# Recurrent cross-attention and a softplus-erf MLP: more filler products at the start, the last stores over two queues, two copies ahead of a conversion step

## The chip, the core and the metric

The kernel runs on one core of a Trainium2 chip. A core has TensorE (PE, matrix products into PSUM), VectorE (DVE), ScalarE (ACT), GpSimd (POOL) and queues that issue DMA transfers, here the sync queue (SPq) and ScalarE's own (ACTq). The metric is the device time of one execution in microseconds; lower is better.

## What is computed

Eight batches with eight heads of 512 tokens by 64 numbers (x) and 32 state rows by 64 (state). Tokens read the states and states read the tokens, each through a softmax. The two results, 544 rows for each batch, are put side by side over the heads into rows of 512 numbers: 4352 rows. These go through a two-layer network.

```python
scores  = scale * x @ state.T;  a  = softmax(scores)      # 512 x 32, for each batch and head
xread   = a @ state
scores2 = scale * state @ x.T;  a2 = softmax(scores2)     # 32 x 512
sread   = a2 @ x
rows    = concat(xread, sread)                            # to (8 * 544, 8 * 64)
h       = rows @ w_in                                     # 512 -> 2048
out     = (h * erf(softplus(h))) @ w_out                  # 2048 -> 512
```

The data are float32, except that both weight matrices arrive as 64-bit floats and are turned into 32-bit ones on the chip.

## The kernel before

**How it is tiled.** Tokens stand in four quarters of 128 (index c), heads in four pairs (index i), the hidden width in four groups of 512 (index g). For tokens, rows @ w_in is not computed as written: for each batch the states are first multiplied with w_in (that is m, of 128 state rows by 2048), and h is then a @ m. For batches 1 to 7 and for the state rows at the end the products are built from seven instead of eight block products (`hidden7`, `project7`); batch 0 uses plain ones (`first0`, `project`).

**Batch 0 and the weights.** All of batch 0 up to line 907 is written out by hand, and `in_order` then ties the instructions of each engine to this order. While batch 0 is computed, 16 blocks of weights are fetched and converted, eight of w_in (kind "i") and eight of w_out (kind "o"). A block takes a DMA into one of three `raw` buffers, two steps on ScalarE (`on_act`, L144 and L146) and three on VectorE (`on_dve`, L147 to L149); the last of the three frees the buffer and so starts the next fetch.

**The opening.** x of batch 0 comes in four transfers, one for each quarter, in turn over ScalarE's and the sync queue (L109). `attention0` transposes the quarters on TensorE in the order 1, 0, 2, 3 (L302), four transposes each, into four PSUM tiles, which ScalarE and VectorE copy to SBUF (L305). One more transpose turns the states (L182, copied by L183). `scored` forms the scores (L197). Then VectorE goes through the softmax of the tokens (L217 to L235) and, at L319, makes `aT`, with the first block's conversion (L147 to L149) in between. `mixed_part` forms half a group of m from the states and w_in (L413) and ScalarE copies it (L415, L416). `first0` is the first product with a (L701); it needs both m and aT. `soft`, `keep_h`, `erf` and `times` make the activation, and `project` the second layer (L541).

**Filler.** `warm(n)` multiplies the identity by itself n times into a PSUM tile that nobody reads at that time (`spare`, L169). It is called before the first transposes and after the scores.

**Around line 809.** ScalarE first does both steps of w_out's block 4, then copies half of m for group 2 (`mixed_part(0, 2, 0, 2, ...)`), and then the transposed states of batches 1 to 7 (`states`, L183). VectorE's steps for that block come later.

**The end.** The last 256 rows are the state rows of all batches. `store7` adds up their results on VectorE (L601) in three pieces: left half of row block 0, whole row block 1, right half of row block 0. For each piece `put_s` issues four stores of 32 rows (L624), since the rows of different batches lie apart in the output. For row block 1 (r == 1) all four went to ScalarE's queue.

Of the kernel before, what the change touches and what calls it, by code (L numbers as in the profile page):

```python
# [16 lines left out]
def kernel(  # L17
# [17 lines left out]
    nc = tc.nc  # L35
# [130 lines left out]
    def warm(n):  # L166

        for _ in range(n):
            last = nc.tensor.matmul(out=spare[:, 0:P], lhsT=ident, rhs=ident, start=True,  # L169
                                    stop=True)  # L170
        return last
# [5 lines left out]
    def states(bs):  # L177


        ps = ps_h.tile([P, len(bs), P], F32, name="h")  # L180
        for k, b in enumerate(bs):
            last = nc.tensor.transpose(out=ps[:, k], in_=st[:, b, :], identity=ident)  # L182
        nc.scalar.copy(st[:, bs[0]:bs[-1] + 1, :], ps)  # L183
        return last
# [5 lines left out]
    def scored(b, xT):  # L190


        s2 = [ps_at.tile([P, S], F32, name="at") for _ in range(2)]
        for i in reversed(range(NI)):
            for e in range(2):
                r, q = slice(D * e, D * e + D), slice(Ns * i, Ns * i + Ns)
                on_pe = nc.tensor.matmul(out=s2[e][q, :], lhsT=st[r, b, q], rhs=xT[r, i, :],  # L197
                                         start=True, stop=True)
        marks.append(on_pe)
        return s2  # L200
# [10 lines left out]
    def states_weights(b, sc, both):  # L211

        aT[b] = keep.tile([P, 2, S], F32, name="aT")
        a = both[:, 0:2].rearrange("p e (k n) -> p e k n", n=Ns)
        m1 = small.tile([P, 2, NC * NI], F32, name="m1")
        for e in range(2):
            nc.vector.transpose(out=both[:, e], in_=sc[e])  # L217
        for e in range(2):
            nc.vector.reduce_max(out=m1[:, e], in_=a[:, e], axis=AX.X)
        for e in range(2):  # L220
            nc.vector.tensor_tensor(a[:, e], a[:, e], over(m1[:, e]), op=ALU.subtract)
            nc.scalar.activation(out=a[:, e], in_=a[:, e], func=ACTF.Exp, scale=scale)
        return a

    def sums(a):
        z1 = small.tile([P, 2, NC * NI], F32, name="z1")
        for e in range(2):
            nc.vector.reduce_sum(out=z1[:, e], in_=a[:, e], axis=AX.X)
        return z1

    def normalise(a, z1):
        nc.vector.tensor_scalar(z1, z1, 1e-9, None, op0=ALU.add)
        nc.vector.reciprocal(z1, z1)
        for e in range(2):
            nc.vector.tensor_tensor(a[:, e], a[:, e], over(z1[:, e]), op=ALU.mult)  # L235

    def largest(sc):
        m2 = small.tile([P, 2], F32, name="m2")
        for e in range(2):
            nc.vector.reduce_max(out=m2[:, e:e + 1], in_=sc[:, e], axis=AX.X)  # L240
        nc.vector.tensor_scalar(m2, m2, -scale, None, op0=ALU.mult)
        return m2

    def weigh_tokens(sc, m2, a2):

        z2 = small.tile([P, 2], F32, name="z2")
        for e in range(2):
            nc.scalar.activation(out=a2[:, e], in_=sc[:, e], func=ACTF.Exp, bias=m2[:, e:e + 1],
                                 scale=scale, accum_out=z2[:, e:e + 1])
        return z2  # L250

    def inverse(z):
        nc.vector.tensor_scalar(z, z, 1e-9, None, op0=ALU.add)
        nc.vector.reciprocal(z, z)

    def turn_weights(a2):
        a2T = att.tile([P, 2, NC, P], F32, name="sc")
        for e in range(2):
            ps = ps_at.tile([P, NC, P], F32, name="at")
            for c in range(NC):  # L260
                nc.tensor.transpose(out=ps[:, c, :], in_=a2[:, e, P * c:P * c + P],
                                    identity=ident)
            nc.scalar.copy(a2T[:, e], ps)
        return a2T
# [3 lines left out]
    def read_tokens(b, a2T, z2, pool=ps_at, name="at"):  # L268


        xt = x_t.pop(b)
        sr = pool.tile([P, 2, D], F32, name=name)
        for e in range(2):
            for c in range(NC):
                for i in reversed(range(NI)):
                    q = slice(Ns * i, Ns * i + Ns)
                    nc.tensor.matmul(out=sr[q, e, :], lhsT=a2T[:, e, c, q],  # L277
                                     rhs=xt[:, c, 2 * i + e, :],
                                     start=(c == 0), stop=(c == NC - 1))
        sn = sn_t[b] = const.tile([P, 2, D], F32, name="sn0") if b == 0 else \  # L280
            st[:, b - 1, :].rearrange("p (e d) -> p e d", e=2)
        for e in range(2):
            nc.vector.tensor_scalar(sn[:, e], sr[:, e], z2[:, e:e + 1], None, op0=ALU.mult)
# [8 lines left out]
    def attention0(between):  # L292

        xt = x_t[0]
        xT = att.tile([P, NI, S], F32, name="xT")
        xp = [ps_o.tile([P, S], F32, name="o%d" % i) for i in range(3)]
        xp.append(ps_h.tile([P, S], F32, name="h"))
        for c in 1, 0, 2, 3:  # L300
            for i in range(NI):
                nc.tensor.transpose(out=xp[i][:, P * c:P * c + P],  # L302
                                    in_=xt[:, c, 2 * i:2 * i + 2, :], identity=ident)
        for i in range(NI):
            (nc.scalar.copy, nc.vector.tensor_copy)[i % 2](xT[:, i, :], xp[i])  # L305
        states(range(1))
        s2 = scored(0, xT)
        between[0]()
        both = att.tile([P, NI, S], F32, name="xT")
        sc = att.tile([P, 2, S], F32, name="sc")  # L310
        a = states_weights(0, s2, both)
        for e in range(2):
            nc.scalar.copy(sc[:, e], s2[e])
        between[1]()
        z1 = sums(a)
        between[2]()
        normalise(a, z1)
        for e in range(2):
            nc.vector.transpose(out=aT[0][:, e], in_=both[:, e])  # L319

        def rest():
            a2 = both[:, 2:4]
            m2 = largest(sc)
            yield
            z2 = weigh_tokens(sc, m2, a2)
            inverse(z2)
            yield
            a2T = turn_weights(a2)
            yield
            read_tokens(0, a2T, z2)  # L330
            yield

        return rest()
# [71 lines left out]
    def mixed_part(b, g, j, parts, copy0=nc.scalar.copy, copy1=nc.vector.tensor_copy):  # L405
        n = gw // parts
        mg = m_t[b, g][:, :, n * j:n * j + n]
        fs = slice(2 * g + j, 2 * g + j + 2 // parts)
        ps = [ps_at.tile([P, gw], F32, name="at")[:, 0:n] for _ in range(2)]
        for i in range(NI):  # L410
            for e in range(2):
                r, q = slice(D * e, D * e + D), slice(Ns * i, Ns * i + Ns)
                nc.tensor.matmul(out=ps[e][q, :], lhsT=st[r, b, q],  # L413
                                 rhs=w_in[r, fs, i, :], start=True, stop=True)
        copy0(mg[:, 0], ps[0])  # L415
        copy1(mg[:, 1], ps[1])  # L416
# [202 lines left out]
    def put_s(r, ot, c=slice(0, d_model)):  # L619
        m = P // Ns  # L620
        for j in range(m):
            r0 = TB * (m * r + j) + S
            queue = nc.scalar if r == 1 or (c.start and j % 2) else nc.sync
            queue.dma_start(out=out[r0:r0 + Ns, c], in_=ot[Ns * j:Ns * j + Ns, c])  # L624

    def tiles(n):
# [4 lines left out]
    def begins(b):  # L631
        return 1 - b % 2
# [44 lines left out]
    def fetch():  # L677
        if len(made) < len(pieces):
            kind, j = w = pieces[len(made)]
            made[w] = (weights_in if kind == "i" else weights_out)(j)  # L680

    def on_act(kind, j, ks=range(2)):
        for k in ks:
            made[kind, j][0][k]()
# [34 lines left out]
    A, Z = slice(0, 2), slice(2, 4)  # L719
    for _ in range(3):  # L720
        fetch()
    warm(5)

    def after_scores():
        warm(28)
        on_act("i", 0)

    def before_sums():
# [3 lines left out]
    def amid_sums():  # L732
        on_dve("i", 0, [2])
        on_act("o", 0, [0])
        m_t[0, 0] = mix.tile([P, 2, gw], F32, name="m")
        mixed_part(0, 0, 0, 2, nc.scalar.copy, nc.scalar.copy)

    rest = attention0((after_scores, before_sums, amid_sums))
    g0 = group()
# [66 lines left out]
    on_dve("i", 4)  # L806
    times(Z, g1)
    on_act("i", 5)
    on_act("o", 4)
    some0(1, g1, range(NC), range(2))  # L810
    m_t[0, 2] = mix.tile([P, 2, gw], F32, name="m")
    mixed_part(0, 2, 0, 2, nc.scalar.copy, nc.scalar.copy)
    for bs in range(1, 5), range(5, B):
        states(bs)
    some0(1, g1, range(1), range(2, 4))
# [99 lines left out]
    for b in range(1, B + 1):  # L915
# [4 lines left out]
        for g, (first, second) in enumerate(groups):  # L920
# [5 lines left out]
            if b + 1 < B:  # L926
# [9 lines left out]
                if g > 1:  # L936
                    o = g - 2 ^ begins(b + 1)
# [56 lines left out]
```

## Time and profile before

| what | value |
|---|---|
| time, median of 3 | 736.64 us (736.46 to 736.71) |
| span of the profiled execution | 734.9 us |
| PE busy | 721.8 us (98%) |
| DVE busy | 523.8 us (71%) |
| ACT busy | 397.0 us (54%) |
| mean DMA rate | 63 GB/s |
| filler at L169 | 66 instructions, 275 ns at the median, up to 582 |
| first useful product (L701) starts at | 23.65 us |
| last addition (L601) starts at | 731.10 us |

PE's share is the time in which at least one product was in flight, not the share of its peak. The filler counts as busy too. The profile's order of time gives each instruction, or a run of equal ones, with its start, its duration, its engine and line, what it writes and reads, and in brackets how long the engine had idled and what ended the wait. Lines of the code are those of the kernel before; in the changed kernel they stand two to four lower.

### The profile page before, as it was taken

To read this page: it belongs to the slowest core of one execution; us is meant where nothing else is said; L and a number is where in the kernel's file an instruction comes from. 1 tells how busy PE (TensorE), PEld (TensorE's weight loads), DVE (VectorE), ACT (ScalarE), POOL (GpSimd) and SP (SyncE) were. 2 spreads that over 40 slices of the span, in tenths; PEclk is the share of its full clock that TensorE was granted. 3 is DMA by queue.
4 is the path that set the end of the run, shared out by engine and by line. 5 is a ranking of instruction groups with operands and counts; after the bars stand their busy time and mean duration, and the time that the engine had idled before them with its cause. 6 is when DMAs were issued, how large, how long until landed. Compare 5 with 4: busy or idle time off the path is not lost.

```text
span 734.9 us, 12066 instructions
## 1 busy us (share of the span) xinstructions
PE 721.8 (98%) x4986; PEld 586.4 (80%) x4986; DVE 523.8 (71%) x765; ACT 397.0 (54%) x499; POOL 0.7 (0%) x6
## 2 busy tenths in 40 slices
PE   7899999999999999999999999999999999999997
PEld 6434435887889888988989888988898899999996
DVE  3987887898698666867688568867686756575423
ACT  3899884657455545654355445654565434443340
POOL 0000000000000000000000000000000000000000
PEclk9999999999999999999999999999999999999999
DMA  7568752331142201510061104210121000000001
GB/s 232 172 202 251 209 110 58 87 58 18 41 89 59 45 11 34 111 29 29 1 144 21 38 1 87 61 35 21 27 62 29 30 1 29 1 29 1 29 1 29
DMA packets 139166, 46.40 MB, mean 63 GB/s; under 512 B 126696, under 2 KB 130536, under 8 KB 139112
## 3 DMA queue, kind: packets, MB, share of 16 engines
q1 hardware_dynamic: 136744, 44.78, 24.5%
q10 hardware_dynamic: 2368, 0.85, 0.6%
q8 instruction: 39, 0.64, 0.4%
q14 instruction: 15, 0.12, 0.1%
HBM read 33.03 MB, written 8.91 MB: 57 GB/s over the span
## 4 chain that ended last, share of the span: by engine, by line
PE 86%; DVE 5%; ACT 3%; issue 1%; DMA 0%; SPq 0%; ACTq 0%; DVEq 0%
PE o L591 48%; PE h L485 25%; PE o L541 5%; PE at L399 2%; PE h L399 1%; PE h L701 1%; PE at L197 1%; PE h L277 1%; DVE hs L493 1%; PE at L413 1%; ACT raw L146 1%; DVE raw L567 1%; ACT L711 1%; DVE s L536 1%; DVE hs L708 0%
## 5 line engine op out<-in xcount | busy, mean ns | idle before, releaser
L591 PE MATMUL o<-w_out,s 128*128 128x256 f32 x480 | 118.2, 380 | 0.9 <-DVE ot L601 0.5
L591 PE MATMUL o<-raw,hs 128*128 128x256 f32 x480 | 117.0, 382 | 0.0
L492 ACT ACTIVATE s<-hs 128x512 f32<-128x512 f32 x120 | 75.3, 630 | 76.0 <-DVE hs L493 75.7
L591 PE MATMUL o<-w_out,hs 128*128 128x256 f32 x480 | 114.0, 380 | 0.2 <-DVE hs L590 0.2
L591 PEld LDWEIGHTS o<-raw,hs 128*128 128x128 f32 x480 | 90.0, 190 | 22.5 <-issue 10.9
L493 DVE TENSOR_TENSOR hs<-hs,h 128x512 f32<-128x512 f32 x90 | 61.7, 687 | 63.7 <-PE h L485 63.7
L591 PEld LDWEIGHTS o<-w_out,hs 128*128 128x128 f32 x480 | 90.6, 190 | 16.8 <-issue 4.2
L591 PEld LDWEIGHTS o<-w_out,s 128*128 128x128 f32 x480 | 84.6, 191 | 9.2 <-DVE ot L601 0.7
L493 DVE TENSOR_TENSOR hs<-s,h 128x512 f32<-128x512 f32 x60 | 41.0, 683 | 68.9 <-PE h L485 68.4
L485 PEld LDWEIGHTS h<-aT,m 128*128 128x128 f32 x672 | 83.9, 192 | 4.7 <-issue 1.4
L485 PE MATMUL h<-aT,m 128*128 128x128 f32 x672 | 84.7, 275 | 0.2 <-ACT s L496 0.2
L536 DVE TENSOR_TENSOR s<-s,hs 128x2048 f32<-128x2048 f32 x30 | 68.5, 2284 | 19.9 <-ACT s L535 19.9
L496 ACT COPY s<-h 128x512 f32<-128x512 f32 x29 | 17.0, 586 | 113.3 <-PE h L485 113.3
L541 PE MATMUL o<-w_out,s 128*128 128x512 f32 x128 | 59.0, 600 | 0.6 <-DVE s L714 0.5
L485 PE MATMUL h<-sy,sx 128*128 128x128 f32 x448 | 59.1, 275 | 0.0
L501 ACT COPY hs<-h 128x512 f32<-128x512 f32 x29 | 17.0, 586 | 76.1 <-PE h L485 76.1
L485 PEld LDWEIGHTS h<-sy,sx 128*128 128x128 f32 x448 | 56.6, 192 | 1.8 <-issue 0.5
L535 ACT ACTIVATE s<-s 128x2048 f32<-128x2048 f32 x30 | 57.4, 1912 | 0.3
L591 PE MATMUL o<-raw,s 128*128 128x256 f32 x240 | 56.8, 379 | 0.0
L541 PEld LDWEIGHTS o<-w_out,s 128*128 128x128 f32 x128 | 23.1, 190 | 30.7 <-issue 25.8
L591 PEld LDWEIGHTS o<-raw,s 128*128 128x128 f32 x240 | 43.5, 190 | 4.8
L492 ACT ACT_TABLE_LOAD x31 | 39.8, 1283 | 0.5
(130 smaller groups left out, 912.1 us busy)
## 6 DMA issues: line engine op xcount, KB each, us to landing
raw<-in_moe_w_in_dram SPq DMA_DIRECT2D x8, 1024.0 KB, 5.6
raw<-in_moe_w_out_dram SPq DMA_DIRECT2D x8, 1024.0 KB, 4.8
xq<-in_x_dram SPq DMA_DIRECT2D x112, 64.0 KB, 2.2
x<-in_x_dram SPq DMA_DIRECT2D x56, 128.0 KB, 2.9
out_dram<-ot SPq DMA_DIRECT2D x18, 256.0 KB, 2.1
sc<-xT SPq DMA_DIRECT2D x112, 32.0 KB, 1.9
out_dram<-ot SPq DMA_DIRECT2D x28, 128.0 KB, 1.7
x<-in_x_dram ACTq DMA_DIRECT2D x2, 256.0 KB, 5.7
```

Source lines behind the costliest of these rows:

```text
L146: lambda: nc.scalar.activation(out=lo, in_=lo, func=ACTF.Copy, scale=2.0 ** -29)], \
L197: on_pe = nc.tensor.matmul(out=s2[e][q, :], lhsT=st[r, b, q], rhs=xT[r, i, :], start=True, stop=True)
L399: nc.tensor.matmul(out=ps[k][e][q, :], lhsT=st[r, b, q], rhs=w_in[r, 2 * g:2 * g + 2, i, :], start=True, stop=True)
L485: last = nc.tensor.matmul(out=bank[:, q], lhsT=lhsT, rhs=rhs, start=(first and i == 0 and k == 0), stop=(i == GF - 1 and k == len(ops) - 1 ...
L492: nc.scalar.activation(out=s[:, k], in_=hs[:, k], func=ACTF.Softplus)
L493: add = lambda o, x, y: nc.vector.tensor_tensor(o, x, y, op=ALU.add)
L496: copy(m1, p)
L501: copy(c11, p)
L535: return (nc.scalar.activation(out=s, in_=s, func=ACTF.Erf), nc.vector.tensor_tensor(s, s, hs, op=ALU.mult))
L536: nc.vector.tensor_tensor(s, s, hs, op=ALU.mult))
L541: nc.tensor.matmul(out=acc[r], lhsT=gT[:, i, P * r:P * r + P], rhs=w_out[:, GF * g + i, :], start=(g == 0 and i == 0), stop=(g == NG - 1 a ...
L591: nc.tensor.matmul(out=acc[bank][:, E2 * c:E2 * c + E2], lhsT=lhs[:, i, :], rhs=rhs[:, g, i, :], start=(first and i == 0 and c == 0), stop ...
```

## The change

It has three parts. Filler: five products before the first transposes become eight, three more come ahead of the third quarter's transposes, 28 after the scores become 32, and five more follow the first half group of m. Their purpose is to keep TensorE at work while it waits. Stores: of the four stores of row block 1 the even ones go to the sync queue, so that both queues share them. ScalarE's order: the second step of w_out's block 4 moves behind the two copies of m, so that m is there earlier. What is computed stays the same.

```diff
         for c in 1, 0, 2, 3:
+            if c == 2:
+                warm(3)
             for i in range(NI):
                 nc.tensor.transpose(out=xp[i][:, P * c:P * c + P],
...
-            queue = nc.scalar if r == 1 or (c.start and j % 2) else nc.sync
+            queue = nc.scalar if j % 2 and (r == 1 or c.start) else nc.sync
...
-    warm(5)
+    warm(8)
 
     def after_scores():
-        warm(28)
+        warm(32)
         on_act("i", 0)
...
         mixed_part(0, 0, 0, 2, nc.scalar.copy, nc.scalar.copy)
+        warm(5)
...
     on_act("i", 5)
-    on_act("o", 4)
+    on_act("o", 4, [0])
     some0(1, g1, range(NC), range(2))
     m_t[0, 2] = mix.tile([P, 2, gw], F32, name="m")
     mixed_part(0, 2, 0, 2, nc.scalar.copy, nc.scalar.copy)
+    on_act("o", 4, [1])
     for bs in range(1, 5), range(5, B):
         states(bs)
```

## The prediction

> **What bounds the kernel now.** I read the chain that ended last, to see which engine sets the end and where it doesn't. It is TensorE nearly everywhere:
>
> ```profile
> PE 86%; DVE 5%; ACT 3%; issue 1%; DMA 0%; SPq 0%; ACTq 0%; DVEq 0%
> ```
>
> No edit touches the steady stretch that makes up this 86%. All four places lie in the first 66 us or the last 7, so I read the order of time there. The opening (columns: start us, duration us, engine, line, operation, tiles; the bracket is idle time before and what ended it; x is the number of instructions, and one 128x128 float32 product is two of them, a transpose one):
>
> ```profile
> 1.35 2.50 PE L169 MATMUL o<-ident 128*128 128x128 f32 x10 [1.35 <-POOL ident masks.py:199]
> ...
> 4.92 0.90 PE L302 MATMUL o<-ident,x 128*128 128x128 f32 x3 [1.06 <-DMA x<-in_x_dram]
> ...
> 7.96 0.90 PE L302 MATMUL o<-ident,x 128*128 128x128 f32 x3 [1.08 <-DMA x<-in_x_dram]
> ...
> 10.15 0.68 DVE L305 COPY xT<-h 128x512 f32<-128x512 f32 x1
> ...
> 10.98 1.96 PE L197 MATMUL at<-xT,st 64*32 64x512 f32 x16 [0.83 <-DVE xT L305]
> ...
> 12.87 8.34 PE L169 MATMUL o<-ident 128*128 128x128 f32 x56
> 13.12 1.31 DVE L217 STREAM_TRANSPOSE xT<-at 128x512 f32<-128x512 f32 x2 [2.29 <-PE at L197]
> ...
> 19.86 1.22 DVE L149 SCALAR_TENSOR_TENSOR w_in<-raw,w_in 128x1024 uint32<-128x1024 uint32 x1
> ...
> 21.22 0.79 PE L413 MATMUL at<-w_in,st 64*32 64x256 f32 x16
> ...
> 22.80 1.29 DVE L319 STREAM_TRANSPOSE aT<-xT 128x512 f32<-128x512 f32 x2
> 23.65 3.67 PE L701 MATMUL h<-aT,m 128*128 128x512 f32 x8 [1.64 <-DVE aT L319]
> ```
>
> The reader is to see a chain: x lands, transposes (L302), copies (L305), scores (L197), and then VectorE, busy without a pause from 13.12 to 24.09, which releases the first useful product at 23.65. TensorE is not the bound after 12.87: its 56 instructions at L169 are filler, and it idles 1.64 us before L701. Whatever makes the transposes and scores end sooner moves the start of VectorE's chain, and with it all that follows. TensorE also ran at half rate for most of this. Two pieces of its order of time, from inside the filler:
>
> ```profile
> 13.67 1.70 PE L169 MATMUL o<-ident 128*128 128x128 f32 x7
> ...
> 16.81 1.39 PE L169 MATMUL o<-ident 128*128 128x128 f32 x11
> ```
>
> The row for L169 gives one instruction 421 ns for most of the slow ones and 275 ns at the fast rate, so starts are (1.70 - 0.421) / 6 = 0.213 us apart before and (1.39 - 0.275) / 10 = 0.1115 us after: nearly twice as fast from about 16.7 us on. The page's clock row stays at 9 throughout and doesn't show this. The transposes also take 421 ns each, the slow figure; the same form at 84 us (L261) takes 272. Scores take 1.96 us here and, at the fast rate,
>
> ```profile
> 528.69 1.09 PE L197 MATMUL at<-xT,st 64*32 64x512 f32 x16
> ```
>
> So the first scores lose 0.87 us to the slow clock.
>
> [...]the clock rose about 3.85 us after the filler began at 12.87, and not earlier, though before that TensorE had work in 68 to 76% of every 3.4 us (busy 2.34, 2.32 and 2.57 us in 3.0 to 6.4, 6.4 to 9.8 and 9.8 to 13.2). [...]L701 starts 0.43 us apart, the full rate. [...]The trace shows that issue time: 0.41 to 0.44 us for a store at L624.
>
> **The change part by part.** Compared in order, the two kernels differ on the engines in nothing but these places.
>
> 1. **Filler before the first transposes, 5 to 8, and 3 between the second and third quarter.** Does it delay them? Eight products are 16 instructions: the second starts at 1.72, each 0.213 later, so the last one ends at about 4.93, when x lands (4.92). The eight transposes that follow take 8 x 0.213 and end at 6.64; three products at the slow rate, 6 x 0.213 = 1.28, end at 7.92, before the next quarter of x (7.96). Cost: nothing, the wait for x hides both. What they give: TensorE streams without a break from 1.35 to 9.9, which is 8.6 us[...] I take full clock by about 6.5.
>  - Transposes after 7.96: eight at 0.1115 instead of 0.213. The last one VectorE's first copy needs (the sixth) starts at 8.52 instead of 9.08 and takes 0.272 instead of 0.421: the copies start 0.70 us earlier. ScalarE's copies gain about 0.60, and with the small copy L183 end at 9.97, still before VectorE's at 10.13. Gain 0.70.
>  - Scores: 1.09 instead of 1.96. Gain 0.87.
>  - VectorE's chain then starts at 13.12 - 1.57 = 11.55. Does another wait take over? ScalarE's first conversion (L144, L146) waits for the weights and ends at 13.55; the exponentials behind it on ScalarE would be due at 16.31 - 1.57 = 14.74. VectorE's L147 and L148 read it at 15.15 and 15.96. None binds. The last of the first three weight blocks has landed by about 16 (DMA traffic falls to nothing there) and is read at 20.41 - 1.57 = 18.84. So the gain stands: 1.57 us.[...]
> 2. **Filler after the scores, 28 to 32.** Queued behind it on TensorE: L413, which needs w_in from L149, done at 21.08 - 1.57 = 19.51. At full rate 64 x 0.1115 = 7.1 us from about 11.2 ends at 18.3. Cost: nothing, hidden by VectorE's conversion.
> 3. **Five after L413.** Queued behind: L701, due at 23.65 - 1.57 = 22.08. L413 ends at about 20.2, the five end 1.1 us later at 21.4. Cost: nothing, hidden by VectorE's chain. They shorten the idle stretch.
> 4. **Copies of m ahead of a conversion step, at 64 us.** The order of time:
>
> ```profile
> 63.10 1.17 ACT L144 ACTIVATE w_out<-raw 128x1024 f32<-128x1024 f32 x1
> ...
> 64.18 1.15 ACT L146 ACTIVATE raw<-raw 128x1024 uint32<-128x1024 uint32 x1
> ...
> 65.22 0.34 ACT L415 COPY m<-at 128x256 f32<-128x256 f32 x1
> 65.46 0.36 ACT L416 COPY m<-at 128x256 f32<-128x256 f32 x1
> ...
> 65.73 0.97 ACT L183 COPY st<-h 128x512 f32<-128x512 f32 x2
> ...
> 66.37 1.98 PE L701 MATMUL h<-aT,m 128*128 128x512 f32 x4 [0.48 <-ACT st L183]
> ```
>
>  m would be ready 1.04 us sooner (its products are done at 63.25), but L701 is released by L183, and ahead of L183 stand the same three instructions in another order. VectorE's L148 needs L146, which would end at about 65.8 instead of 65.3; it starts at 66.44 behind L147. Gain and cost: nothing; L183 hides it.
> 5. **Last stores.** Before:
>
> ```profile
> 728.77 3.60 SPq L624 DMA_DIRECT2D out_dram<-ot  x6
> ...
> 730.10 2.77 ACTq L624 DMA_DIRECT2D out_dram<-ot  x6
> 731.10 0.42 DVE L601 TENSOR_TENSOR ot<-ot,o 128x256 f32<-128x256 f32 x1 [0.71 <-PE o L591]
> ```
>
>  The last half rows are ready at 731.52. ScalarE's queue is then still issuing its fourth whole-row store (to 731.9), and its last two start at 731.98 and 732.43. With two of the four moved to the sync queue, ScalarE's queue is free at 731.0; the sync queue issues its two after its first four (to 730.5) and is free at 731.4. Both then wait for 731.52, and the last issue starts at about 731.97. Gain 0.45. Unknown is how four stores at once land (1.5 to 1.9 us before): bounds 0.3 and 0.5.
>
> Does the early gain last? From 20 us to 160 us no compute engine's wait was ended by a DMA, and the transfers are started by buffers that come free, so all of it should shift together. Sum: 1.57 + 0.45 = 2.02, so 736.64 - 2.02 = **734.6 us**.
>
> **The rivals.** *The clock rises late, at the scores*[...]: 0.87 + 0.45, so 735.3.[...] *The clock rises where it did*: then eight more filler instructions end at 21.9, L413 and the five new products behind it end at 23.85, and L701 is 0.2 late: 736.64 + 0.2 - 0.45 = 736.4.[...] *The clock rises early and falls again* in the idle stretch from 18.3 to 19.5 and 21.4 to 22.1: L701's first eight instructions at half rate would take 3.4 us more, 736.64 - 2.0 + 3.4 = 738.0, slower than before. Against it: from 20.0 to 23.4 TensorE was busy for only 2.0 us, and the clock held.
>
> **How the numbers follow.** Forecast 70%, late rise 12%, no earlier rise 12%, fall 6%. The forecast spreads from 734.1 (the scores' and the stores' gains both a little larger) to 735.0; with the late rise the range reaches 736.0, and leaves out 18%. A change of 0.2% is 1.47 us, so faster means below 735.17: nearly all of the forecast and a third of the late rise, 0.70. Slower is the fall: 0.06. The rest, 0.24, is within.
>
> **What would show it.** In the profile after: transposes in the third quarter 272 ns instead of 421; scores in 1.09 us; VectorE's L217 at 11.5; L413 released by L149 and no longer behind filler; L701 at 22.1, still released by aT; L183 near 65.7 - 1.6; last stores issued by 732.4 less the shift, on both queues. Transposes still at 421 and L217 after 12.5 would prove the first step wrong; L701 at 0.85 us apart, the third.

## The result, and the profile after

The changed kernel takes 734.86 us (median of 6 runs, 734.77 to 734.94), beside 736.67 for the kernel before: 1.81 us less. The ratio is 0.9973, with a 95% interval of 0.996 to 0.9986. The forecast was 734.6.

The order of time of the changed kernel, opening. Lines of the code stand two to four lower than before (L304 is L302, L415 is L413, L703 is L701, L321 is L319):

```profile
1.35 3.65 PE L169 MATMUL o<-ident 128*128 128x128 f32 x16 [1.35 <-POOL ident masks.py:199]
...
4.84 0.51 PE L304 MATMUL o<-ident,x 128*128 128x128 f32 x3
...
5.98 0.83 PE L169 MATMUL o<-ident 128*128 128x128 f32 x6
7.84 0.55 PE L304 MATMUL o<-ident,x 128*128 128x128 f32 x3 [1.03 <-DMA x<-in_x_dram]
...
10.18 1.09 PE L197 MATMUL at<-xT,st 64*32 64x512 f32 x16 [0.65 <-DVE xT L307]
11.21 7.41 PE L169 MATMUL o<-ident 128*128 128x128 f32 x64
11.46 1.31 DVE L217 STREAM_TRANSPOSE xT<-at 128x512 f32<-128x512 f32 x2 [1.42 <-PE at L197]
...
19.56 0.79 PE L415 MATMUL at<-w_in,st 64*32 64x256 f32 x16 [0.94 <-DVE z L232]
...
20.27 1.38 PE L169 MATMUL o<-ident 128*128 128x128 f32 x10
...
21.14 1.30 DVE L321 STREAM_TRANSPOSE aT<-xT 128x512 f32<-128x512 f32 x2
21.99 3.67 PE L703 MATMUL h<-aT,m 128*128 128x512 f32 x8 [0.33 <-DVE aT L321]
```

The reader is to see that the eight first products end as x lands, that three transposes take 0.51 us where they took 0.90, that scores take 1.09 us where they took 1.96, and that VectorE's chain (L217) starts 1.66 us sooner. The first useful product keeps this lead (23.65 to 21.99), and so does the last addition, some 707 us later (731.10 to 729.45). L415 waited 0.94 us for VectorE, so none of the new filler stood in its way; L703 is still released by aT. The first transposes already run at the fast rate (0.51 us for three, 0.90 before): the trace has the granted clock at 1.00 from 4.73 us on, just ahead of the landing of x at 4.84.

At 64 us, ScalarE and the product behind it:

```profile
62.50 0.37 ACT L417 COPY m<-at 128x256 f32<-128x256 f32 x1
62.75 0.39 ACT L418 COPY m<-at 128x256 f32<-128x256 f32 x1
...
63.01 1.18 ACT L146 ACTIVATE raw<-raw 128x1024 uint32<-128x1024 uint32 x1
...
64.07 0.96 ACT L183 COPY st<-h 128x512 f32<-128x512 f32 x2
...
64.71 1.98 PE L703 MATMUL h<-aT,m 128*128 128x512 f32 x4 [0.49 <-ACT st L183]
```

L183 and the product start 1.66 us earlier than before (65.73 to 64.07, 66.37 to 64.71), which is the lead of the opening, and the product waits for L183 as it did. The new order itself moved nothing. The end:

```profile
727.11 3.70 SPq L626 DMA_DIRECT2D out_dram<-ot  x8
...
728.44 2.33 ACTq L626 DMA_DIRECT2D out_dram<-ot  x4
729.45 0.42 DVE L603 TENSOR_TENSOR ot<-ot,o 128x256 f32<-128x256 f32 x1 [0.71 <-PE o L593]
```

The last issue is over at 730.81 on the sync queue, 1.36 us after the last addition began; before it was over at 732.87 on ScalarE's, 1.77 after. That is 0.41 us. But the span, from 734.9 to 733.0, fell by only about 0.2 more than the addition's lead of 1.65.

### The profile page after: what moved, and what is told of

It is laid out like the page before. It is cut to its first block, busy times and chain, and to the rows that moved or that the text cites. A ratio compares the mean times of both kernels' runs of the same rounds, so it can differ in the third digit from the quotient of the medians.

```text
span 733.0 us, 12127 instructions
## 1 busy us (share of the span) xinstructions
PE 721.4 (98%) x5016; PEld 587.0 (80%) x5016; DVE 523.7 (71%) x765; ACT 397.0 (54%) x499; POOL 0.7 (0%) x6
## 4 chain that ended last, share of the span: by engine, by line
PE 87%; DVE 6%; ACT 2%; issue 1%; DMA 0%; SPq 0%; DVEq 0%; ACTq 0%
PE o L593 48%; PE h L487 26%; PE o L543 6%; PE at L401 2%; PE h L401 1%; PE h L703 1%; PE at L197 1%; PE at L415 1%; PE h L277 1%; DVE hs L495 1%; DVE raw L569 1%; DVE s L538 1%; DVE s L716 0%; DVE hs L710 0%; DMA out_dram<-ot 0%
## 5 line engine op out<-in xcount | busy, mean ns | idle before, releaser
L593 PEld LDWEIGHTS o<-w_out,hs 128*128 128x128 f32 x480 | 90.6, 190 | 16.8 <-issue 4.2
```

Source lines behind the costliest of these rows:

```text
L593: nc.tensor.matmul(out=acc[bank][:, E2 * c:E2 * c + E2], lhsT=lhs[:, i, :], rhs=rhs[:, g, i, :], start=(first and i == 0 and c == 0), stop ...
```

## The experiments

Each kernel was timed beside the kernel before on the same chip; figures are medians. The groups of experiments ran on different chips, on which the kernel before took 736.59 to 736.74 us (736.67 beside the changed kernel), so a difference to the changed kernel is known to some 0.1 us only. Of each run the mean granted clock of TensorE is on record too. It counts the time before the first change of the clock as full (the kernel before reads 1.00 from 13.2 to 16.6 us, where its products start 0.213 us apart, and they do so 0.1115 apart after 16.8), so it shows falls and not late rises; by my estimate 3.41 us at 0.50 take about 0.002 from it (3.41 x 0.50 / 735).

**The parts, each alone on the kernel before.** The four filler edits:

```diff
-    warm(5)
+    warm(8)
...
+            if c == 2:
+                warm(3)
...
-        warm(28)
+        warm(32)
...
         mixed_part(0, 0, 0, 2, nc.scalar.copy, nc.scalar.copy)
+        warm(5)
```

> Kernel before with the four filler edits alone (8, 3, 32 and 5 products); stores and ScalarE's order as before. My theory: the early rise of TensorE's clock gives nearly the whole gain; VectorE's L217 starts near 11.5 us instead of 13.12 and the time is 1.6 to 1.7 us below the kernel before (735.0). Rival, that the stores give a good part as forecast (0.45) and the filler the rest: 1.3 to 1.4 us below.

Measured: 735.15 us beside 736.74, ratio 0.9973 (0.9962 to 0.9983). L217 starts at 11.56. The filler is worth 1.6 us of the 1.81.

```diff
-            queue = nc.scalar if r == 1 or (c.start and j % 2) else nc.sync
+            queue = nc.scalar if j % 2 and (r == 1 or c.start) else nc.sync
```

> Kernel before with the last stores over both queues alone. From the two traces I expect 0.2 us less than the kernel before: the last issue comes 0.4 us earlier, and 0.2 of it is lost[...]. The forecast's figure was 0.45. Rival, that the stores give nothing: 0.0.

Measured: 736.42 us, 0.32 less at the median, ratio 0.9994 (0.9986 to 1.0002). The interval holds 1, so these times alone don't prove a gain. That the filler alone stays 0.29 above the whole change (0.22, each against its own kernel before) points the same way. The traces settle it: from the start of the last addition (L601) to the end of the span it is 3.8 us in the three with the old stores (kernel before, filler alone, ScalarE's order alone) and 3.5 to 3.6 in the two with the new ones (changed kernel, stores alone). The stores are worth 0.2 us.

```diff
-    on_act("o", 4)
+    on_act("o", 4, [0])
...
     mixed_part(0, 2, 0, 2, nc.scalar.copy, nc.scalar.copy)
+    on_act("o", 4, [1])
```

> Kernel before with the copies of m ahead of the conversion step alone. My theory: no change, within 0.1 us, since the first product of group 2 is still released by the copy of the states at L183, which ends at the same time. Rival, that m's earlier copy lets TensorE start group 2 sooner: up to 0.5 us less.

Measured: 736.66 us, ratio 0.9996 (0.9988 to 1.0004): no change that can be told. In its trace the first product of group 2 is again released by L183.

**The first eight alone.**

```diff
-    warm(5)
+    warm(8)
```

> Kernel before with eight instead of five filler products before the first transposes and nothing else (28 after the scores, none elsewhere). My theory: [...]the clock rises at about 4.7 us and the whole filler gain is there: 1.6 to 1.7 us below the kernel before. Rival 1, that the three products between the quarters are needed to keep the clock up: it falls before the scores, scores take 1.96 us, gain at most 0.8. Rival 2, that the first product needs the five fillers ahead of it: L701 starts 0.85 us apart.

Measured: 736.62 us, from 736.09 to 737.86, ratio 0.9997 (0.9989 to 1.0005). Eight alone bring nothing at the median and make the time uneven. The granted clock was 0.994 to 0.998 in all 13 runs, lower in each of them than in the six runs of the changed kernel, where it was 0.999 or 1.000. The profiled run, at 737.47 one of the three slowest, shows where. It is cut at the points where its granted clock changes (10.11, 13.52, 23.76 and 27.18), and the time between and before them into equal lengths (columns: stretch, length, TensorE busy with its instructions, granted clock, DMA share, GB/s):

```profile
6.70:10.11 3.41, 1.53 (x10) 1.00 1.10 346
10.11:13.52 3.41, 3.26 (x22) 0.50 1.05 417
13.52:16.93 3.41, 3.41 (x33) 1.00 0.46 185
16.93:20.35 3.42, 2.38 (x22) 1.00 0.00 0
20.35:23.76 3.41, 1.61 (x18) 1.00 0.68 202
23.76:27.18 3.42, 3.42 (x5) 0.50 0.26 105
```

The clock had risen by 7.91, where three transposes took 0.55 us, 0.85 at 5.79. It was 0.50 from 10.11 to 13.52 and from 23.76 to 27.18, and 1.00 from 13.52 to 23.76. In the stretches just ahead of the two at 0.50, TensorE was busy for 1.53 and 1.61 us. The scores took 1.96 us, as in the kernel before, and the first products

```profile
22.93 5.37 PE L701 MATMUL h<-aT,m 128*128 128x512 f32 x8 [1.64 <-DVE aT L319]
```

5.37 us in place of 3.67. Both of my rivals were right in this run and my theory wrong: with the eight the clock rose before the third quarter, but without the rest of the filler it did not stay up. Which part of the rest matters is the question of the next runs.

**Taking one place away from the changed kernel.**

```diff
-    warm(8)
+    warm(5)
```

> Changed kernel with five instead of eight products before the first transposes. My theory[...]: TensorE then streams without a break only from 4.9 to about 9.9 us[...]. Times spread between 735.0 and 736.5, more than the changed kernel's 0.2 us; median near 735.8. Rival[...]: no spread, 0.2 to 0.6 above the changed kernel.

Measured: 735.30 us, 14 runs from 734.77 to 736.55: the spread that I expected, with a lower median. The profiled run is the slowest of them: transposes still at 0.90 us for three, scores at 1.96, L217 at 13.18; the 64 filler instructions that start at 12.93 took 8.11 us, the changed kernel's 7.41. No run shows a fall (0.999 or 1.000 in all 14).

```diff
-            if c == 2:
-                warm(3)
```

> Changed kernel without the three products ahead of the third quarter's transposes. My theory: the clock rises by about 6.6 us in about half of the executions and then falls again before the scores[...]; scores take 1.96 us in most, and the time is 0.8 to 1.6 above the changed kernel (735.7 to 736.5). Rival, that eight products are enough: same as the changed kernel, 734.9.

Measured: 734.95 us, but in two heaps: 8 runs from 734.77 to 734.98 and 5 from 735.81 to 736.44, nothing between. I expected most of them in the higher heap. The profiled run is of the lower one, at a clock of 1.000. The record tells the heaps apart: the granted clock was 0.999 or 1.000 in all eight runs of the lower heap, 0.995 in four of the higher and 0.998 in the fifth. So the clock fell in the higher heap; where it fell, no trace shows.

```diff
-        warm(5)          # after the first half group of m
```

> Changed kernel without the five products after the first half group of m. My theory: in some 8 of 10 executions [...]the clock falls, and the first products at L701 run at half rate for up to 3.4 us; time 0.8 to 1.7 above the changed kernel in those (735.7 to 736.6), none above in the others. Rival[...]: 734.9.

Measured: 734.95 us, again two heaps: 7 runs from 734.75 to 735.05 and 3 from 735.95 to 736.21. I expected 8 in 10 in the upper one. The granted clock was 1.000 in all seven and 0.998 in the three. In the profiled run, from the lower, TensorE waited 0.95 us ahead of L415 and 1.64 ahead of L703, and the granted clock stayed at 1.00:

```profile
17.68:21.09 3.41, 1.69 (x25) 1.00 0.26 30
21.09:24.51 3.42, 2.55 (x6) 1.00 0.70 277
```

Here TensorE was busy for 1.69 of 3.41 us and the next stretch was at 1.00; in the run with eight alone it was 1.61, and the next stretch was at 0.50. What parts the two heaps, these traces don't show.

The kernel before has this gap too (TensorE waits 1.64 us ahead of L701), and its runs fall into two heaps as well: of the 96 taken beside these experiments, 8 took 738.0 to 738.2 us at a clock of 0.998, the others at most 736.9 at 0.999 or 1.000. Of the 20 runs with all four filler edits (changed kernel, filler alone, swapped order below) none shows a fall. So the new filler probably removes these longer executions too, but no trace of one was taken, and 20 runs are few. The step from 28 to 32 was never taken back alone.

**No filler after the scores, and none at all.**

```diff
-        warm(32)
...
-        warm(5)          # after the first half group of m
```

> Changed kernel without any filler after the scores and after the first half group of m (the eight and the three ahead stay). My theory: the clock rises early, VectorE's chain starts at 11.5 as in the changed kernel, but TensorE is nearly idle from 11 to 22 us, the clock falls in every execution and L701 (L703 there) starts at half rate; 1.5 to 2.6 us above the changed kernel (736.4 to 737.5), with little spread between early and late. Rival, that VectorE and ScalarE hide the slow products: under 0.5 us above.

Measured: 737.02 us (736.43 to 737.78), 2.2 above the changed kernel. The granted clock was 0.990 to 0.993 in all 13 runs, so it fell in every one. The stretches of the profiled run, cut at the changes, and the first products:

```profile
10.08:13.49 3.41, 1.09 (x16) 1.00 1.05 391
13.49:27.15 13.66, 6.26 (x22) 0.50 0.39 132
```

```profile
22.12 6.17 PE L703 MATMUL h<-aT,m 128*128 128x512 f32 x8 [1.20 <-DVE aT L321]
```

The granted clock was 0.50 from 13.49 to 27.15; the first products took 6.17 us instead of 3.67.

With every call of `warm` taken out of the changed kernel:

> Changed kernel with no filler anywhere. My theory: transposes and scores at half rate as in the kernel before (1.6 us) and the first products at half rate as well (1.5 to 2.6): 3.1 to 4.2 us above the changed kernel, 738 to 739. Rival, that the kernel before's own filler was worth nothing: 736.3, the kernel before less the stores' gain.

Measured: 738.49 us (737.78 to 739.12), 3.6 above the changed kernel, inside the expected 3.1 to 4.2.

**One DMA for each piece of the last rows.**

```diff
-        for j in range(m):
-            r0 = TB * (m * r + j) + S
-            queue = nc.scalar if j % 2 and (r == 1 or c.start) else nc.sync
-            queue.dma_start(out=out[r0:r0 + Ns, c], in_=ot[Ns * j:Ns * j + Ns, c])
+        rows = out.rearrange("(b t) e -> b t e", t=TB)[m * r:m * r + m, S:S + Ns, c]
+        queue = nc.scalar if r == 1 else nc.sync
+        queue.dma_start(out=rows, in_=ot[:, c])
```

> Changed kernel with each piece of the last rows stored by one DMA in place of four (three issues in all, over the two queues). My theory: what is left after the last addition is one issue of about 0.4 us and one landing of 1.5 to 2.0; the second issue on each queue (0.45 us) goes, so 0.3 to 0.5 less than the changed kernel, 734.4. Rival, that landing and not the issue sets the end: the same as the changed kernel within 0.1, or slower if one DMA of four times the size lands later.

Measured: 739.29 us, ratio to the kernel before 1.0034 (1.0022 to 1.0046), 4.4 above the changed kernel. The last addition starts at 729.46, as in the changed kernel, and the last issue is over at 730.5, so it is all in the landing. From 730.5 to 735.5 the DMA engines were busy 0.24 of the time, at 72 GB/s; the changed kernel's last stores, from 729.9 to 732.1, made 0.47 and 139 GB/s. Of the 16 engines that the profile counts, that is the work of about four (0.24 x 16), beside seven or eight (0.47 x 16). What makes the merged transfers slower, no run shows.

**A better order of the quarters.** By the changed kernel's trace the fourth quarter of x lands before the third (7.2 and 7.8 us).

```diff
-        for c in 1, 0, 2, 3:
-            if c == 2:
+        for c in 1, 0, 3, 2:
+            if c == 3:
                 warm(3)
```

> Changed kernel with the third and fourth quarters' transposes in the other order, since the fourth quarter of x lands at 7.2 us by the trace and the third at 7.8. My theory: with the clock up, four transposes (0.44 us) leave the path, but the states' copy, whose data land at 9.1, then holds the scores: 0.1 to 0.3 below the changed kernel. Rival: the copies, not the transposes, set the start of the scores, no change.

Measured: 734.55 us (734.41 to 734.66), ratio to the kernel before 0.9971 (0.9959 to 0.9982); 0.31 below the changed kernel's median (0.27, each against its own kernel before), with no run of either in the other's range. L217 starts at 11.24 instead of 11.46.

```diff
     for c in range(NC):
         (nc.scalar, nc.sync)[c % 2].dma_start(
             out=x_t[0][:, c], in_=x[0, :, P * c:P * c + P].rearrange("h p d -> p h d"))
-    for e in range(2):
-        nc.sync.dma_start(out=st[:, 0, D * e:D * e + D], ...
+        if c == 1:
+            for e in range(2):
+                nc.sync.dma_start(out=st[:, 0, D * e:D * e + D], ...
```

> As the swapped order, and the states' two small loads issued ahead of the fourth quarter of x. My theory: the states land in time and the full 0.44 us leaves the path: 0.35 to 0.45 below the changed kernel, 734.45. Rival: the fourth quarter, issued 1 us later, lands after the third, and nothing or less than the swap alone is gained.

This stands on top of the swapped order. Measured: 735.79 us (735.57 to 737.31), 0.9 above the changed kernel and 1.2 above the swapped order: the rival was right, and the loss was larger than it said. The profiled run is the slowest of the 13. In it the fourth quarter came late, TensorE waited 1.92 us,

```profile
8.92 0.79 PE L305 MATMUL o<-ident,x 128*128 128x128 f32 x3 [1.92 <-DMA x<-in_x_dram]
```

and from 9.08 on the granted clock was 0.50 (stretches cut at the changes):

```profile
5.67:9.08 3.41, 1.49 (x13) 1.00 1.17 306
9.08:12.49 3.41, 2.58 (x17) 0.50 1.06 411
12.49:15.91 3.42, 3.42 (x26) 0.50 0.70 284
```

The scores then took 1.96 us, and L217 started at 13.96, where the swapped order had 11.24. Its transposes waited until 8.92 for the load, where the swapped order began them at 7.67: 1.25 us later at the load became 2.7 at L217. This is the worst case and not the usual one. Nine of the 13 runs took 735.57 to 735.90 at a clock of 0.999 or 1.000, three 736.28 to 736.45 at 0.998, and the profiled one 737.31 at 0.995. The fall of the clock thus goes with the spread and not with the median, whose loss of 1.2 us against the swapped order is about the lateness of the load alone.

## Why the prediction held, step by step

1. *The filler hides in the waits for x, and the clock rises early.* Right. The eight end with the landing of x and the three before the third quarter. The clock rose at 4.73 us. That it would be up by about 6.5 was an estimate of mine; nothing in the trace of the kernel before showed it. L217 moved 1.66 us, forecast 1.57. The copies gained 0.80 (forecast 0.70; the third quarter landed 0.12 earlier in this run, 7.84 for 7.96), the scores and what waits for them 0.86 (forecast 0.87). In the traces of the filler alone, of the swapped order, without the five and without filler after the scores, whose loads and filler up to there are the same, the clock rose later: three transposes of the first two quarters took 0.85 to 0.88 us, and from 7.6 us on 0.49 to 0.55:

```profile
4.93 0.85 PE L304 MATMUL o<-ident,x 128*128 128x128 f32 x3
```

 This is from the swapped order, against 0.51 in the changed kernel. It costs little, because the quarter that follows is awaited anyway: L217 started at 11.56, 11.24, 11.43 and 11.59 in these runs. All six runs of the changed kernel lie within 0.17 us.
2. *32 after the scores, and five after L415, cost nothing.* Right: L415 idled 0.94 us for VectorE after the 32. That they don't only cost nothing but are needed, the forecast had not priced: without both of them 2.2 us are lost.
3. *The copies of m move nothing.* Right, by the order of time and by the run with this edit alone.
4. *The stores, 0.45.* This term was too large: 0.2 by five traces, 0.2 to 0.3 by the medians of two comparisons. The step that gave it, the last issue, was right: 0.41 us earlier. What it took as unchanged is the landing, for which I named a lower bound of 0.3, and that was too high: from issue to landing the stores took 1.5, 1.8 and 2.0 us at the least, the median and the most, where I knew 1.5, 1.7 and 1.9. That accounts for some 0.1 of the 0.2 us lost. Where the rest went, no run shows. In the run with one DMA for each piece the landing outweighed what was saved at the issue (4.4 us more in all).
5. *The early gain lasts to the end.* Right: 1.66 us at L703, 1.65 at the last addition.

Of the rivals, none came about in the changed kernel, but "the clock falls again" is a real danger of this opening: it happened in every run with the first eight alone (0.994 to 0.998) and with no filler after the scores (0.990 to 0.993), and in some runs when the three or the five were missing or a load came late. The price that I set on it, 3.4 us, was too high: L703 took 2.5 us more without filler after the scores (6.17 for 3.67) and 1.7 more with eight alone, because the granted clock was 1.00 again from 27.15 and 27.18 us, while these products ran.

The sum 1.57 + 0.45 = 2.02 became 1.66 and 0.2 by the trace, 1.81 by the medians. The opening gave 0.09 more than forecast and the stores 0.25 less: the two errors go in opposite directions, so it is in part luck that the total came out as near as it did.

## What to carry to other kernels

Where TensorE waits in the opening for loads or for other engines, filler products that fit into the wait cost nothing here, and they are worth having (1.6 us) when products on the path follow; fit them to the landing times and look at every wait, since one uncovered stretch (no filler after the scores) took back all that the change gives. Judge such an edit by the spread of many runs and not by the median alone: with the three or the five missing, 8 of 13 and 7 of 10 runs were about as good as the changed kernel's, and the others lost 0.9 to 1.6 us. For the same reason, see where a profiled run stands among the others before its trace is taken to explain the median. Before a store or a load is moved to save its issue, ask how late it will land (half of the 0.41 us saved at the issue was lost there), and whether a transfer behind or ahead of it becomes late (1.25 us here).

## What the runs showed of the hardware that I had not expected

In two traces TensorE's granted clock fell with no wait of 2 us ahead of it. In the one with the late load it was 0.50 from 9.08 to 15.91; the longest wait shortly ahead of that was 1.92 us (before 8.92). With eight alone the longest wait shortly ahead of the fall at 10.11 was 1.08 us (before 7.91), and of that at 23.76 it was 1.64 (before 22.93).

In the 3.41 us ahead of a fall, TensorE was busy for 1.61 and 1.53 us (eight alone), 1.49 (the late load) and 1.09 (no filler after the scores). After stretches of this length with 1.69 (without the five) and 2.38 us (eight alone) it was 1.00. Two stretches of the kernel before:

```profile
9.89:13.31 3.42, 2.59 (x20) 1.00 1.05 416
20.13:23.55 3.42, 1.87 (x26) 1.00 0.40 79
```

The second, with 1.87 us, is followed by the full rate too (L701 took 3.67 us for eight). The first lies ahead of the rise; its clock column reads 1.00 because it ends before the first change of the trace. With 2.59 us busy in it, products still started 0.213 us apart at 13.67, and the clock rose at 16.72. With the late load it was still 0.50 after 2.58 us (9.08 to 12.49) and rose at 15.91, after 3.42 of 3.42. With eight alone it rose at 13.52 after 3.26, and at 27.18 after 3.42. These are single executions and don't make a rule.

The time of the rise is not fixed by the code: in two traces with the same opening as the kernel before, the same 56 filler instructions took 7.86 us (the stores alone) and 8.61 (ScalarE's order alone), beside 8.34.
